# An mLSTM scan followed by a gated layer: the written-out sequence of steps is laid anew

## Chip, cores, metric

One core of one Trainium2 chip. The metric is the device time of one execution in microseconds. The kernel before takes 530.96 us, the median of 3 runs (530.82 to 531.62).

## What is computed

The reference has two stages. The first is a recurrent attention (mLSTM) over 4 batches, 8 heads, 768 steps and head size 40. The second is a gated feed-forward layer over the 3072 x 320 outputs of the first. All arrays are fp32 (the weights come as 64-bit numbers).

```python
for t in range(S):
    m_new = np.maximum(f_gate[:, :, t] + m, i_gate[:, :, t])
    f_stab = np.exp(f_gate[:, :, t] + m - m_new)
    i_stab = np.exp(i_gate[:, :, t] - m_new)
    C = f_stab * C + i_stab * outer(vt, kt)
    n = f_stab * n + i_stab * kt
    y[:, :, t] = sigmoid(o_gate[:, :, t]) * (C @ qt) / max(abs(n . qt), 1)
x = y as (B*S, H*D)                       # 3072 x 320
out = (sigmoid(x @ w_gate) * (x @ w_val)) @ w_out     # 320 -> 1536 -> 320
```

## The kernel before

The scan is done in 6 chunks of 128 steps, for 4 batches each: 24 units, counted u = 4c + b. For each unit the kernel loads q, k, v and the output gate, builds a 128 x 1024 decay matrix (`e`: exponentials on ScalarE; `em`: GpSimd masks it, L468), turns q and k round, forms scores (`b`, TensorE) and multiplies them into the decay matrix (`bm`, VectorE, L729). It gathers the values (`c`, L693), adds the carried state (`ci`, `cf`, `cs`), normalises (`cv`, `cg`, `cr`, `cx`), transposes the result (`d`) and splits it into a high and a low half (`dx`, `dy`). The state is carried by `z`, `zm`, `zd` and `za`. Units 0 to 7 turn q and k on TensorE (`a`, `ah`, and `aq`, which spreads q over a block mask, L620). Later units turn them on VectorE (`a`, L633), split them (`ah`, `al`) and send them through DRAM (`as`, then `s` and `aq`).

The gated layer works in 103 tiles (`t0` to `t102`), each with one 128-wide slice of the 1536 columns and 256 or 512 tokens. A tile has 16 matmuls up (`t`, L895), a tanh on ScalarE (`ta`, L908), the gate on VectorE (`tg`, L911), a split into high and low (`th`, `tl`; L916 or L918, and L922) and 6 or 12 matmuls down (`p`, L933). Every product is made as three products of high and low halves.

The weights come as 64-bit words and are decoded on the chip, in 30 parts (`wg`, `wv`, `wr`, `w3` to `w29`). ScalarE starts a part (`a`, L492). VectorE makes three steps on it (`b`: L497, L501 and L505), of which each reads what the one before wrote. Then `d` makes the high half (ScalarE or VectorE), `e` the low half (VectorE or GpSimd; L546, L550, L552), and `f` starts the load of a later part into a staging buffer (L513, L517, L520).

Nothing in the program plans at run time. Each step is put under a key with `put` (as `put(key + "b", ...)`), and a written string `ORDER` says which key comes next:

```python
for word in ORDER.split():
    if word == "/":
        other("pa")
        continue
    key, _, n = word.partition("*")
    for _ in range(int(n or 1)):
        f, args = todo[key].pop(0)
        f(*args)
```

So the order in the string is the order in which each engine's queue is filled; engines wait for each other by semaphores alone. A "/" swaps the next PSUM bank of two. A second table, `PARAM["eng"]`, says for a step which engine makes it ('v' VectorE, 'a' ScalarE, 'p' GpSimd). The SP queue issues almost all transfers, in the order of the string too.

Of the kernel before, what the change touches and what calls it, by code (L numbers as in the profile page):

```python
# [33 lines left out]
        'aq4.0': 'v', 'ah4.1': 'a', 'aq4.1': 'p', 'aq4.2': 'v', 'bd4': 'v', 'cr4': 'p', 'dx4': 'a', 'aq5.0': 'v',  # L34
        'ah5.1': 'a', 'bk5': 'p', 'zd5.1': 'p', 'tl1': 'p', 'tl2': 'p', 'tl10': 'v', 'arg': 'a', 'w24e': 'v',
        'w27d': 'a', 'za4.0': 'p', 'zm5.0': 'a', 'za5.0': 'p', 'zm5.1': 'a', 'ah6.0': 'a', 'ah6.2': 'v', 'aq6.2': 'v',
        'bd6': 'p', 'za6.0': 'v', 'zd6.1': 'v', 'ah7.0': 'a', 'ah7.1': 'v', 'ah7.2': 'a', 'bk7': 'p', 'cx7': 'p',
        'zm7.0': 'v', 'zd7.0': 'v', 'za7.0': 'v', 'aq8.0': 'a', 'aq8.2': 'v', 'bd8': 'v', 'cr8': 'v', 'cx8': 'p',
        'zm8.0': 'v', 'zd8.0': 'p', 'zm8.1': 'v', 'zd8.1': 'p', 'za8.1': 'v', 'aq9.0': 'a', 'e9a': 'p', 'dx9': 'v',
        'zm9.0': 'v', 'zd9.0': 'p', 'za9.0': 'p', 'zd9.1': 'v', 'aq10.0': 'a', 'cr10': 'v', 'zm10.1': 'a',  # L40
        'zd10.1': 'v', 'za10.1': 'v', 'aq11.0': 'v', 'aq11.2': 'a', 'e11a': 'a', 'bd11': 'p', 'bk11': 'p',
# [1119 lines left out]
```

## Time and profile before

| what | value |
|---|---|
| median of 3 runs | 530.96 us (530.82 to 531.62) |
| the profiled execution's own time | 532.02 us |
| its span, first to last instruction | 530.30 us |
| granted TensorE clock, mean | 0.99 |
| TensorE busy | 510.8 us (96%) |
| VectorE busy | 346.1 us (65%) |
| ScalarE busy | 196.6 us (37%) |
| GpSimd busy | 159.6 us (30%) |
| moved | 75.55 MB, mean 142 GB/s |

The profile is of one execution. A view by line groups instructions of one kind and gives the sum, the mean of one, and what ended the idle time before them. A view by stretch gives the busy time of each engine in it, with the number of instructions in brackets. In a view in order of time, each row is an instruction (or several alike) with its start and its duration in us. Durations of one engine can overlap a little, since an instruction may begin before the one ahead of it has written its last element.

### The profile page before, as it was taken

What the parts mean: (1) busy time and instruction counts of PE and PEld (TensorE: products, weight loads), DVE (VectorE), ACT (ScalarE), POOL (GpSimd) and SP (SyncE); (2) the same over time, 40 slices, a digit from 0 to 9 for tenths busy, and PEclk for the clock granted to TensorE, in tenths of its full rate; (3) what the DMA queues carried; (4) which work ended last, traced back from release to release, by engine and by line L of the source; (5) the groups of instructions that cost most, each with busy time, mean ns of one, the idle gap of its engine ahead of it and who ended that gap; (6) DMA issues with size and microseconds to landing.
All of it is one profiled execution on the core that took longest, in us unless ns stands there. A gap on an engine that the chain in (4) does not pass through costs nothing.

```text
span 530.3 us, 12170 instructions
## 1 busy us (share of the span) xinstructions
PE 510.8 (96%) x4667; PEld 461.5 (87%) x4667; DVE 346.1 (65%) x794; ACT 196.6 (37%) x514; POOL 159.6 (30%) x233
## 2 busy tenths in 40 slices
PE   7687899999999999999999999999999999999997
PEld 6476787888999999998888888888888888999997
DVE  5999999999867746675566667555655543533323
ACT  4565656773332333341243332333242140122211
POOL 4524232333643243231233414233222032111020
PEclk9978999999999999999999999999999999999999
DMA  9973866774796989496977789987777633000001
GB/s 201 240 179 128 220 154 189 175 173 75 168 198 128 228 166 200 115 163 144 196 147 170 137 191 176 206 160 176 144 171 159 132 96 88 26 27 1 12 1 39
DMA packets 227578, 75.55 MB, mean 142 GB/s; under 512 B 207040, under 2 KB 215424, under 8 KB 227520
## 3 DMA queue, kind: packets, MB, share of 16 engines
q1 hardware_dynamic: 226432, 74.51, 64.2%
q8 instruction: 37, 0.61, 0.5%
q10 hardware_dynamic: 1088, 0.26, 0.3%
q14 instruction: 21, 0.17, 0.1%
HBM read 57.61 MB, written 17.14 MB: 141 GB/s over the span
## 4 chain that ended last, share of the span: by engine, by line
PE 79%; DVE 14%; DMA 4%; issue 2%; SPq 1%; ACT 0%; DVEq 0%; ACTq 0%
PE pg L895 44%; PE po L933 22%; PE av L693 3%; PE in L744 2%; PE s L723 2%; DVE dc L505 2%; PE cs L848 2%; DVE dc L497 1%; DMA st<-in_moe_w_gate_dram 1%; DMA q<-in_q_dram 1%; DVE dc L501 1%; PE s L718 1%; PE xt L813 1%; DVE qbd L620 1%; DMA qk<-scr0q 1%
## 5 line engine op out<-in xcount | busy, mean ns | idle before, releaser
L908 ACT ACTIVATE sg<-pg 128x256 f32<-128x256 f32 (+1 forms) x103 | 48.2, 468 | 226.3 <-PE pg L895 202.4
L895 PE MATMUL pg<-xh,wh 128*128 128x256 f32 (+1 forms) x412 | 112.6, 340 | 3.1 <-ACT sg L908 2.7
L911 DVE SCALAR_TENSOR_TENSOR sg<-sg,pg 128x256 f32<-128x256 f32 (+1 forms) x103 | 53.8, 522 | 91.9 <-ACT sg L908 52.2
L895 PE MATMUL pg<-xl,wh 128*128 128x256 f32 (+1 forms) x412 | 109.6, 333 | 0.0
L895 PE MATMUL pg<-xh,wl 128*128 128x256 f32 (+1 forms) x412 | 109.4, 333 | 0.0
L922 POOL TENSOR_TENSOR gl<-sg,gh 128x256 fp32r<-128x256 f32 (+1 forms) x52 | 49.9, 960 | 152.9 <-ACT gh L916 72.2
L933 PE MATMUL po<-oh,gh 128*128 128x320 f32 x288 | 88.4, 319 | 0.0
L933 PE MATMUL po<-ol,gh 128*128 128x320 f32 x288 | 87.9, 315 | 0.0
L933 PE MATMUL po<-oh,gl 128*128 128x320 f32 x288 | 86.6, 317 | 0.0
L895 PEld LDWEIGHTS pg<-xh,wh 128*128 128x128 f32 x412 | 70.0, 190 | 9.0 <-ACT sg L908 3.3
L895 PEld LDWEIGHTS pg<-xl,wh 128*128 128x128 f32 x412 | 70.9, 190 | 6.3 <-issue 0.6
L895 PEld LDWEIGHTS pg<-xh,wl 128*128 128x128 f32 x412 | 70.1, 190 | 5.0
L895 PE MATMUL pg<-xl,w 128*128 128x256 f32 (+1 forms) x206 | 59.8, 330 | 0.0
L933 PEld LDWEIGHTS po<-oh,gh 128*128 128x128 f32 x288 | 53.4, 189 | 3.6
L933 PEld LDWEIGHTS po<-ol,gh 128*128 128x128 f32 x288 | 53.7, 188 | 2.8
L933 PEld LDWEIGHTS po<-oh,gl 128*128 128x128 f32 x288 | 53.1, 188 | 3.5 <-DVE gl L922 0.6
L895 PE MATMUL pg<-xh,w 128*128 128x256 f32 (+1 forms) x206 | 53.4, 330 | 0.1
L729 DVE TENSOR_TENSOR d<-s,d 128x384 f32<-128x384 f32 (+1 forms) x66 | 32.9, 507 | 27.3 <-PE s L723 22.1
L447 ACT ACTIVATE d<-d,at 128x128 f32<-128x128 f32 x136 | 42.4, 391 | 0.0
L916 ACT ACTIVATE gh<-sg 128x256 fp32r<-128x256 f32 (+1 forms) x53 | 26.1, 493 | 37.0 <-DVE sg L911 25.9
L468 POOL TENSOR_SCALAR_AFFINE_SELECT d<-d 128x1024 f32<-128x1024 f32 x22 | 27.0, 1229 | 39.0 <-ACT d L447 27.4
L895 PEld LDWEIGHTS pg<-xl,w 128*128 128x128 f32 x206 | 36.6, 189 | 2.3
(174 smaller groups left out, 745.9 us busy)
## 6 DMA issues: line engine op xcount, KB each, us to landing
d<-mscr SPq DMA_DIRECT2D x22, 512.0 KB
k<-in_k_dram SPq DMA_DIRECT2D x24, 160.0 KB
v<-in_v_dram SPq DMA_DIRECT2D x24, 160.0 KB
o<-in_o_gate_dram SPq DMA_DIRECT2D x24, 160.0 KB
st_o<-in_moe_w_out_dram SPq DMA_DIRECT2D x12, 320.0 KB
scr0q<-qt SPq DMA_DIRECT2D x32, 120.0 KB
scr1q<-qt SPq DMA_DIRECT2D x32, 120.0 KB
out_dram<-ob SPq DMA_DIRECT2D x24, 160.0 KB
```

The source lines that it names most:

```text
L447: nc.scalar.activation(d[:, h, :], d[:, h, :], AF.Exp, bias=at[:, c, b * H + h : b * H + h + 1], scale=-1.0)
L468: nc.gpsimd.affine_select(out=d, in_=d, pattern=[[0, H], [1, L]], compare_op=ALU.is_ge, fill=0.0, base=0, channel_multiplier=-1)
L505: nc.vector.scalar_tensor_tensor(ti, st[:, :, 0], 29, ti, ALU.logical_shift_right, ALU.bitwise_or)
L693: nc.tensor.matmul(dst[xs], lhs[:, xs], rhs, start=True, stop=True)
L723: nc.tensor.matmul(ps[g][:, m, :], ks[: 3 * D, h0 + m, :], qs[: 3 * D, h0 + m, :], start=True, stop=True)
L729: nc.vector.tensor_tensor(x, ps[g][:, :nh, :], x, ALU.mult)
L895: nc.tensor.matmul(pg[x], w[:, a, fs] if a < 2 else w[:, fs], y[c][:, a, n0:n1], start=first, stop=a == 2 and y is xl)
L908: nc.scalar.activation(sg[0], pg[0], AF.Tanh, scale=0.5)
L911: nc.vector.scalar_tensor_tensor(sg[0], sg[0], 1.0, pg[1], ALU.add, ALU.mult)
L916: nc.scalar.activation(gh[u][:, :nt], sg[0], AF.Copy)
L922: E('gl0' if c == 0 else 'gl', f'tl{n}').tensor_tensor(gl[u][:, :nt], sg[0], gh[u][:, :nt].bitcast(F32), ALU.subtract)
L933: nc.tensor.matmul(po[t], g[c, j, t0][:, (t - t0) * P : (t - t0 + 1) * P], o[:, j, :], start=j == 0 and first, stop=j == NF - 1 and last)
```

## The change

No function changes, and no step is added or taken out. Two tables differ. `ORDER` holds the same 4513 steps in another sequence: in 3677 words in place of 3647, with 39 swaps of the PSUM bank in place of 36. `PARAM["eng"]` gives another engine to 262 of the instructions: 78 go from GpSimd to VectorE and 72 back, 61 from VectorE to ScalarE and 51 back. They are splits of the gated layer (`th`, `tl`), state updates (`zm`, `zd`, `za`), low halves of weights (`w..e`), copies and normalisations. The matmuls are the same and in nearly the same sequence.

The two hunks are long; their first lines show what they are. In the lines of before, three steps of one decode often stand close (`w7b*2 w5e w7b`, `wrb*2 iq wrb`); in the new lines other VectorE steps stand between.

```diff
--- before.py
+++ after.py
@@ -26,71 +26,71 @@
     'eng': {
         'bh0': 'v', 'bh1': 'v', 'bh2': 'v', 'gl': 'v', 'gl0': 'v', 'arg0': 'a', 'q31': 'v', 'bl2': 'p', 'ca': 'v',
         'qb00': 'v', 'qb01': 'v', 'qb02': 'v', 'qb10': 'v', 'qb11': 'v', 'qb12': 'v', 'cm0': 'a', 'arg1': 'a',
-        'cm1': 'a', 'cp00': 'a', 'cp02': 'v', 'qb2': 'v', 'ro': 'v', 'xd0': 'v', 'bk0': 'p', 'cx0': 'p', 'bk1': 'p',
-        'cr1': 'v', 'cx1': 'v', 'wve': 'v', 'w3e': 'v', 'w4e': 'p', 'w5e': 'v', 'w6e': 'p', 'w7e': 'v', 'w8e': 'v',
-        'w10e': 'v', 'w11e': 'v', 'w13e': 'v', 'w16e': 'p', 'w17e': 'v', 'w18e': 'v', 'w19e': 'p', 'w20e': 'v',
-        'w21e': 'v', 'w23e': 'v', 'w25e': 'v', 'aq2.0': 'v', 'ah2.1': 'a', 'aq2.1': 'v', 'ah2.2': 'a', 'bk2': 'p',
-        'cr2': 'p', 'cx2': 'v', 'zm2.1': 'a', 'aq3.0': 'v', 'ah3.1': 'a', 'aq3.1': 'v', 'cr3': 'p', 'zm3.1': 'v',
...
+        'cm1': 'a', 'cp00': 'a', 'cp02': 'a', 'qb2': 'v', 'ro': 'v', 'xd0': 'v', 'bk0': 'p', 'cx0': 'p', 'bk1': 'p',
+        'cr1': 'v', 'cx1': 'p', 'wve': 'v', 'w3e': 'p', 'w4e': 'p', 'w5e': 'v', 'w6e': 'v', 'w7e': 'v', 'w8e': 'v',
+        'w10e': 'v', 'w11e': 'v', 'w13e': 'v', 'w16e': 'v', 'w17e': 'p', 'w18e': 'p', 'w19e': 'v', 'w20e': 'v',
+        'w21e': 'p', 'w23e': 'v', 'w25e': 'v', 'aq2.0': 'v', 'ah2.1': 'a', 'aq2.1': 'v', 'ah2.2': 'a', 'bk2': 'p',
+        'cr2': 'p', 'cx2': 'p', 'zm2.1': 'a', 'aq3.0': 'v', 'ah3.1': 'a', 'aq3.1': 'v', 'cr3': 'p', 'zm3.1': 'v',
...
@@ -102,158 +102,159 @@
 }
 ORDER = """
 w26f w25f w29f w28f w21f iw it if ii lq0 iq lk0 ib iq x0 iq x1 v1 lk1 ir lq1 ig v0 ig lv0 ig ia iq gc lo0 sp00 gc
-iac g x2 ex00 iq sp01 mk00 tr01 ig gc iq tr02 cp01 is tr00 wva wga ex01 ic igs qb01 tr11 lk2 sp10 cp00 wgb mk01 lq2
-ie cp11 cp02 sp11 lv1 qb00 ex11 lo1 bd0 qb11 tr12 sc01 x3 qb02 ex10 wgb mk11 sc00 ti01 ld2 tr10 wgb x4 / sc02 cp12
-mk10 lq3 ct0 ti00 sc11 cp10 gcs qb12 bd1 ti02 c0 bk1 ti11 v2 qb10 bk0 sc12 cg0 a2.2 iq cv0 ah2.2 z1 cv0 wvb cv0 wvb
-sc10 ct1 cr0 lk3 wvb wra iq wgf a2.1 ti10 ah2.1 ti12 c1 cx0 zm1.0 gc g wgd / d0 wrb*2 iq wrb dx0 wge cg1 wvd w3f
-dy0 wrd cv1*3 cr1 aq2.2 zm1.1 cx1 wre w5a / d1 g w3a a2.0 ld4 g*2 dx1 iq w3b ah2.0 g w3b e2 iq dy1 / a3.0 w3b t0
-w5b e2a wrf t0 wve iq lo3 t0*2 w5b t0*2 ld3 t0 w3d w5b t0 e2m t0 lv2 t0 w7a t0*2 g t0 w5d t0 lo2 t0*2 w3e h0 ta0
-lv3 aq2.1 w6a t1 h0c t1 tg0 t1*3 ah3.0 th0 im w7b*2 w5e w7b p0 w4a / z0 w6b w7d w6b p0 t1 lk6 t1 w6b t1 ct3 t1*2
-b2.2 gs bd2 w4b w6d w4f t1 w4b t1*2 w4b t1 w5f t1 w6e t1 tl0 w7f zm0.0 ta1 bm2.2 wvf e3a zm0.1 tg1 t2*2 p0 aq2.0
-t2*2 p0 t2 / a3.1 w7e th1 t2*2 ah3.1 t2 tl1 t2 g t2 e3 g a3.2 p0 t2 ah3.2 t2*3 g t2 g b2.0 ta2 e3m e4 aq3.0 p0 b2.1
-aq3.1 bm2.0 t3*2 w4d t3 t2 bm2.1 w8a b3.1 aq3.2 bk2 w11a bd3 t3 c2 bm3.1 ct2 v3 w8b w4e w8b p1 w8b b3.0 cv2*2 w8d
-w8f cg2 t3*2 bm3.0 b3.2 bk3 w9a lq4 cv2 tg2 z2 cr2 bm3.2 w6f t3 w11b c3 zm2.1 zm2.0 w8e w9b p1*2 cv3 th2 w9b t3*2
-w9b p1*2 tl2 cx2 d2 cg3 w9d w9f t3 cv3 lk4 p2 cv3 dx2 t3 w11b t3 cr3 t3 w12a w11b t3 ld5 t3*2 z3 dy2 w11d w11f
...
+iac g x2 ex00 iq sp01 mk00 tr01 ig gc iq tr02 cp01 is tr00 ex01 wga mk01 lo1 g tr11 cp02 igs sp11 bd0 cp11 lq2 ex11
+qb01 gcs tr12 wgb iq lk2 sp10 qb02 cp00 wgb cp12 qb00 sc01 ex10 qb11 lv1 tr10 wgb sc00 wra mk10 x4 ti01 cp10 sc02
+ie wva ld2 ti00 v2 mk11 wgf ti02 ct1 c0 wrb bd1 ct0 x3 qb10 bk1 wgd iq cg0 sc10 cv0 wvb ic sc11 qb12 cv0 wvb a2.1
+cv0 iq wvb bk0 ah2.1 z1 ti11 sc12 zm1.1 lk3 ti10 a2.0 cr0 wvd ti12 c1 wrb zm1.0 cx0 gc wrb wge g ah2.0 w3f a2.2 cg1
+iq ah2.2 cv1 wrd iq cv1*2 d0 lv2 wre iq aq2.2 lq3 dx0 cr1 w3a dy0 e2a w3b cx1 d1 g w3b v3 g w5a z0 w3b wve w3d wrf
+dx1 ld3 w5b w3e w7a zm0.1 lo2 dy1 t0 ld4 t0 w5b t0 lv3 w6a aq2.0 t0*2 e2 aq2.1 t0*4 w5b t0*3 a3.0 w7b t0 w5d t0 w6b
+e2m t0*2 g w7b ta0 tg0 t1*2 zm0.0 t1 th0 w6b im ah3.0 bd2 w5e w7b w4a t1 w6b t1 w4f t1 w7d t1*2 lo3 t1 w4b t1*2 w6d
+tl0 t1 h0 a3.1 w4b t1 g t1 ah3.1 t1 p0 w4b e3 t1 / b2.2 h0c aq3.1 w7f p0*2 w5f g b2.0 w6e ta1 lk6 e3a g p0 t2 w6f
+t2 tg1 t2*3 w7e t2*2 ct2 t2*2 e3m t2 w8a bm2.0 t2*2 p0 th1 t2 bm2.2 t2 / a3.2 w4d aq3.0 t2 b2.1 ah3.2 w4e tl1 p1
+w8b ta2 b3.1 bd3 bm2.1 ct3 w9a w8b p0 t3 bk2 e4 c2 bm3.1 w9b aq3.2 p1 w8b p1 b3.0 cv2 cg2 w8d w8f cv2 w11a p1 w9b
+bk3 t2 bm3.0 b3.2 lq4 t3 cv2 w11b p1 z2 cr2 wvf bm3.2 tg2 zm2.0 c3 w11b cx2 w9b th2 t3*2 cv3 zm2.1 w11b t3 w9f t3
+tl2 t3*2 lk4 d2 cv3 cg3 ld5 t3*2 cv3 dx2 t3 w8e t3*2 cr3 t3 g p2 dy2 w12a t3 p2 w9d p2 w12b t3 cx3 ta3 d3 w12b w9e
...
```

## Rows read from the trace of the kernel before

**Rows 1.** The page's busy time of engines: us, share of span, instructions.
```profile
PE 510.8 (96%) x4667; PEld 461.5 (87%) x4667; DVE 346.1 (65%) x794; ACT 196.6 (37%) x514; POOL 159.6 (30%) x233
```

**Rows 2.** Busy time by stretch; columns in its first row.
```profile
core 0: us, PE busy (x) PEld busy (x) DVE busy (x) ACT busy (x) POOL busy (x), PEclk, DMA share, GB/s
0.00:10.00 10.00, 7.50 (x35) 6.35 (x35) 4.72 (x12) 4.00 (x10) 4.40 (x21) 1.00 0.91 206
10.00:20.00 10.00, 8.88 (x112) 6.67 (x112) 9.61 (x24) 6.09 (x24) 6.05 (x11) 1.00 1.00 230
20.00:30.00 10.00, 5.88 (x88) 5.37 (x89) 9.56 (x25) 7.02 (x22) 2.01 (x2) 0.75 0.69 187
...
120.00:140.00 20.00, 19.87 (x180) 16.98 (x179) 19.05 (x41) 7.59 (x20) 8.02 (x12) 1.00 0.57 113
...
160.00:200.00 40.00, 40.00 (x440) 39.56 (x439) 26.57 (x69) 12.72 (x39) 13.06 (x24) 1.00 0.87 179
...
320.00:360.00 40.00, 40.00 (x345) 35.09 (x344) 23.38 (x50) 11.19 (x29) 12.04 (x18) 1.00 0.92 186
```

**Rows 3.** TensorE's waits over the span: us in total, times, longest.
```profile
PE xt L813 <- DVE x L791: 4.0, 1, 4.0
PE pg L895 <- ACT sg L908: 2.7, 2, 2.2
PE s L718 <- DVE d L729: 2.5, 1, 2.5
...
PE in L744 <- DMA qk<-scr0q: 0.5, 1, 0.5
```

**Rows 4.** The chain that ended last, in order of time: start, us, what.
```profile
57.88 6.97 DMA st<-in_moe_w_gate_dram
...
305.40 5.32 DMA qk<-scr0q
...
386.24 3.50 PE pg L895 x15
...
514.23 1.91 PE pg L895 x16
516.14 0.73 PE po L933 x5
```

**Rows 5.** VectorE in order of time, 35 to 37 us: start, duration, instruction.
```profile
35.02 0.42 DVE L505 SCALAR_TENSOR_TENSOR dc<-st,dc 128x256 int32<-128x256 int32 x1
35.36 0.42 DVE L497 TENSOR_SCALAR dc<-dc 128x512 f32<-128x512 f32 x1
35.81 0.43 DVE L501 TENSOR_SCALAR dc<-dc 128x512 int32<-128x512 int32 x1
36.27 0.69 DVE L505 SCALAR_TENSOR_TENSOR dc<-st,dc 128x512 int32<-128x512 int32 x1
36.88 0.17 DVE L699 COPY dl<-d 128x8 f32<-128x8 f32 x1
```

**Rows 6.** All engines in order of time, near 70 us.
```profile
69.96 1.24 POOL L468 TENSOR_SCALAR_AFFINE_SELECT d<-d 128x1024 f32<-128x1024 f32 x1 [2.77 <-ACT d L447]
...
70.17 1.31 DVE L620 TENSOR_TENSOR qbd<-qk,bmask 80x256 f32<-80x256 f32 x1
```

**Rows 7.** VectorE groups by shape, 10 to 140 us: busy, mean ns, idle before.
```profile
L505 DVE SCALAR_TENSOR_TENSOR dc<-st,dc 128x512 int32<-128x512 int32 x12 | 11.4, 948 | 0.2
...
L505 DVE SCALAR_TENSOR_TENSOR dc<-st_o,dc 128x320 int32<-128x320 int32 x12 | 5.8, 486 | 0.2
```

**Rows 8.** Line L729 over the span: ns least/median/most, first and last start.
```profile
L729 DVE TENSOR_TENSOR d<-s,d x66: 380/548/560, 39.8 to 452.4; 128x384 f32<-128x384 f32 x44, 128x256 f32<-128x256 f32 x22
```

**Rows 9.** VectorE in order of time, two landmarks.
```profile
127.39 0.49 DVE L505 SCALAR_TENSOR_TENSOR dc<-st_o,dc 128x320 int32<-128x320 int32 x1
...
130.65 0.69 DVE L911 SCALAR_TENSOR_TENSOR sg<-sg,pg 128x512 f32<-128x512 f32 x1
```

More of the change, by code (lines that the diff above doesn't have):

```diff
@@ new lines @@
+ta19 tg19 e10a p18 t20 zm7.1 lk10 t20 zm7.0 t20 th19 t20 p17 lv10 t20*4 p18 t20*2 p18 t20 za7.1 t20 o3 t20 tl19
+t20*3 cr7 p19 ta20 p19*2 al10.0 p18*2 tg20 t21 as10.3 t21 p19 cx7 t21 bd8 th20 as10.1 t21*2 e10 t21 as10.0 tl20
+t21*8 aq9 t21*2 p20 aq9 ta21 p20 / ci8 as10.2 tg21 p19*2 cf8 zd8.1 p20 th21 t22 e10m t22 a11.0 t22*6 dy6 t22*4
+za7.0 t22*2 tl21 t22 / b8.0 bk8 ta22 p20 b8.1 oh2 t22 p21 bm8.1 p20 t23*2 tg22 p21 t23*2 p20 th22 t23 bm8.0 / b8.2
+tl22 t23*2 s9 zd8.0 p21 t23*2 s9 t23 p22 bd10 t23 s9 ah11.0 t23*2 a10.1 t23 s9 t23 p22 t23 ta23 p21 al11.0 p21 d7
@@ new lines @@
+cv15 p53 cv15 aq16 p52 cg15 ta54 p53 t54 aq16 cv15 p52 p53 tg54 cr15 p53 p52*4 cx15 p52*2 p53 th54 p53*3 tl54 d15
+z15 dx15 p54 zm15.0 p54 lk18 dy15 p54*2 t55 bk16 t55 p54 bd17 zd15.0 t55*2 a18.0 t55 p54 t55 zd14.1 oh9 t55 a17.1
+t55 oh8 t55*2 o8 ah17.1 t55*2 as17.3 al17.1 t55 o9 t55*2 ld18 z16 za15.0 ta55 s16 p53 za14.1 t55 p53 zm15.1 t56
+tg55 za15.1 p54 p53 bk17 zm16.1 t56*2 th55 t56 p54*2 t56 tl55 t56*2 oh10 t56*2 o10 t56*2 lv17 t56*2 s16 t56*2
+as17.6 ci16 ta56 lo18 p55 zd16.0 aq17 p54 t56 zd16.1 as17.4 p55 t57 tg56 t57*2 cf16 p55 p54 as17.7 p55 zm16.0 p54
@@ new lines @@
+th59 p58*3 ld19 p57 p58 e18m t60 tl59 t60 p58 t60*2 bd18 t60*2 v19 t60 za16.0 t60*4 p58 t60*2 b17.0 ta60 b17.2
+bm17.0 t60 p59*2 bm17.2 t61 cg16 t61*2 tg60 t61 b17.1 t61 th60 bm17.1 s18 t61*2 aq18 ci17 tl60 s18 p59 aq18 p59
+zd17.1 p60 s18 t61*2 zd17.0 cf17 s18 t61 z17 lv19 za16.1 cr16 a20.0 t61 zm17.0 t61 a19.0 cx16 t61 lq21 t61*2 za17.0
+lo19 t61 ta61 p59 c17 ah20.0 tg61 ct17 t62 ct18 cs17 p59*3 e19a ah19.0 p59*2 cv17 t62 al19.0 p60*4 p59 as19.2 p60
+p59 th61 t62*2 cv17 ah19.1 t62 as19.0 tl61 cv17 cg17 / d16 t62 dx16 t62 aq18 t62*2 al19.1 t62 cr17 t62*2 p61*2
@@ new lines @@
+ah23.1 t73 s22 cv20 p71*2 cv20 s22 al23.1 bm21.1 t73 p71 s22 t73 cv20 tl72 t73 s22 e22m t73 as23.5 t73 bm21.2 t73*3
+p71*2 zd19.0 p71*3 cr20 p71*2 t73*2 lo23 cx20 / c21 ta73 as23.7 e23a t73 aq22 cs21 t74*2 tg73 t74 p72 ct21 p72
+as23.6 t74 e23 t74 cg21 aq23 t74 th73 t74 aq23 t74 aq23 t74 d20 lv23 t74 dx20 t74 p71 as23.4 t74 tl73 t74 aq22
+t74*2 dy20 p72*2 ta74 p72 cv21 p72 cv21 p72 p73 p72*4 t75 t74 p72 t75 tg74 t75*2 p73 th74 t75*2 cv21 tl74 t75 cr21
+p73 t75*4 za19.0 cx21 p74 t75 za19.1 t75*2 v23 t75 p73*2 ta75 p73*2 t75 d21 tg75 t76 dx21 t76*3 p73*2 t76*2 p73
@@ new lines @@
+p84 tg85 p84 t86*2 th85 t86*4 tl85 t86*9 p84 p85 ta86 t86 p84 p85 tg86 p85 t87*2 th86 t87*4 tl86 t87*2 p85 t87*7
+p86*2 ta87 p86 t87 p85*2 tg87 t88*4 th87 t88*2 tl87 t88*9 p86*2 ta88 t88 p86 p87 tg88 p87 t89*2 th88 t89*4 tl88
+t89*9 p87*2 ta89 p88*2 t89 p87*2 tg89 t90*4 th89 p88 t90 tl89 p88 t90 p88 t90*9 p88 t90 ta90 p89*3 tg90 p89 t91*2
+th90 t91*5 tl90 t91*9 p89 ta91 p89 p90*2 tg91 p90 t92*2 th91 t92*4 tl91 t92 p90 t92 p91 t92*8 p91 ta92 p91 p90*2
+tg92 p91 t93*2 th92 t93*4 tl92 t93*4 p92 t93*5 p91 t93 ta93 p92*2 oh21 p91 tg93 p92 t94*2 th93 t94*4 tl93 t94*10
@@ L257 @@
+p100 p101*2 th102 p101*2 tl102 p101*2 p102*5 oh22 p102 oh23 o22 o23
 """
```

255 lines of the change are left out of this document (115 added, 140 removed), and 120 rows, old and new, of the table PARAM.

## The prediction

> **What bounds the kernel now.** Start with the busy shares [rows 1]: TensorE is taken for 96% of the span, VectorE for 65%. A mean over stages says little, so the table by stage comes next [rows 2]. From 10 to 140 us VectorE is busy for 125 of 130 us (three of the ten stretches of that time are shown, from 95.3 to 96.1%), while TensorE is down to 5.88 of 10 us at 20 to 30 us and still short of full at 120 to 140. From 160 us on it is the reverse: TensorE is full and VectorE is busy for 26.57 of 40 us. So there are two kernels in one: an opening of some 130 us whose pace VectorE sets (weight decode, masks, score products), and then about 395 us in which TensorE runs through the gated layer. The list of TensorE's waits [rows 3] says the same: the large ones (4.0, 2.7, 2.5 us) end on VectorE or on ScalarE behind it, all in the opening; after 140 us there is one of 0.5 us. The chain of waits [rows 4] gives TensorE's spacing once it is full: 3.50 us for 15 matmuls of 512 columns (0.233 each), 1.91 for 16 of 256 (0.119), 0.73 for 5 of 320 columns (0.146). No matmul is added or dropped, so the part behind the opening costs the same before and after unless a wait appears in it. What the change is worth is therefore what VectorE saves ahead of the same TensorE step in the opening.
>
> **Three terms make VectorE's time in the opening.** The last weight word is decoded at 127.39 us [rows 9]; in the written order 273 VectorE instructions stand ahead of it. Each priced at the undisturbed duration of its shape, less the 0.08 us by which neighbours overlap, they sum to 95.9 us. 53 neighbours of which the second reads what the first wrote add 53 x 0.11 = 5.8 us. Stalls behind GpSimd add 15.7 us, and idle time, half of it in the first 10 us, 10.0. That is 127.4, the measured time; so the terms can be trusted to about 1 us. The same sums, step by step, for the change:
>
> **Dependent neighbours: -4.2 us.** Look at the starts in the VectorE rows of the decode [rows 5]. The 128x256 L505 starts at 35.02 and takes 0.42, and the unrelated L497 behind it starts at 35.36, 0.08 us before that end. L501 reads what L497 wrote and starts 0.03 us after its end (35.36 + 0.42, then 35.81), and so does L505 at 36.27. The unrelated L699 again starts 0.08 us early. A dependent neighbour thus costs 0.11 us. The written order has 54 of them ahead of the gate of tile 15 (130.65 us, [rows 9]), 30 of them the decode's L497-L501-L505; the new one has 16. 38 x 0.11 = 4.2 us. Since VectorE has no slack there, nothing hides this. The steps put between the pairs are other VectorE steps that were due anyway, so they cost nothing; a decode's result comes one step later (some 0.5 us), and ScalarE's copy behind it can wait that long, since ScalarE is busy for only 6 to 7 of 10 us [rows 2].
>
> A rule of the Trainium skill speaks against this term: "VectorE: DVE Perf Modes", section "The DRAIN you can't avoid", has every operation followed by a pipeline flush before the next starts, and says that a semaphore between two costs nothing extra. By it a dependent neighbour would cost no more than another and the sum would lose its 4.2 us. The 0.11 us of [rows 5] disagrees, so the rule is kept as a rival only.
>
> **Engine choices: -0.7 us.** The steps that change engine nearly cancel on VectorE. Ahead of the gate of tile 15 it has 276 instructions in place of 278 and the same sum without pairs (97.8 against 97.9 us); ahead of the gate of tile 13 it has 1.3 us less (86.1 against 87.4). I take the middle, 0.7; the ends are 0 and 1.3. GpSimd gets 53 tensor instructions ahead of the last decode in place of 47 (36.9 us against 34.1), and it is idle for more than half of the opening [rows 2]. Their later finish (a 128x320 subtraction takes GpSimd longer than VectorE) falls on weight parts and masks which TensorE reads several us later by the order, and GpSimd's queue has nothing urgent behind them. TensorE's own list is nearly the same: the matmul work ahead of the gates of tiles 13 and 15 goes from 79.3 to 80.1 and from 92.0 to 92.5 us. Those extra 0.5 to 0.8 us would come on top; I leave them out.
>
> **Stalls behind GpSimd: -1.5 us.** One case in full [rows 6]: GpSimd's mask runs from 69.96 to 71.20; VectorE's 80x256 product (0.41 us undisturbed) starts at 70.17 and takes 1.31, to just behind that end. It shows in the groups too: L505 on 128x512 has a mean of 948 ns, on 128x320 486 [rows 7], where the widths alone would give 690 for the first. Instructions that read a matmul's bank are never caught: L729 stays within 380 and 560 ns in all its 66 cases [rows 8]. Over all VectorE instructions before 127.39 us, 29 run over the usual duration of their shape by more than 0.1 us, 15.7 us together, 0.54 each. How many are caught after the change cannot be read from the trace. The nearest evidence is which VectorE step the order puts next behind each GpSimd step. Before the last decode that is one that works in SBUF alone (and so can be caught) 25 times with 18.3 us of GpSimd time before, and 25 times with 16.3 us after. 15.7 x 16.3 / 18.3 = 14.0, so 1.7 us less; I take 1.5. The ends lie far off: alignment to a tenth of a us decides each case and an order holds it only roughly, so anything from half of the stalls gone (-7.8) to 45 of the 53 GpSimd instructions catching one (+8.6) has to be kept.
>
> **The queues of SP and ScalarE.** Loads and saves move by a few places: the two q loads ahead of the second weight block, the mask loads. The opening's weight loads wait for a staging buffer that VectorE's decode frees (one such load, 6.97 us from its issue, is in the chain [rows 4]), so they come earlier with VectorE and I cost them at nothing as long as the transfer engines have room: 0.69 to 1.00 of their time is taken between 10 and 30 us, 0.57 between 120 and 140 [rows 2]. If that room is gone, it is the rival on transfers below.
>
> **The clock.** Between 20 and 30 us the granted clock is 0.75 on average, that is part of the stretch at 1.2 in place of 2.4 GHz, while TensorE waits (5.88 of 10 us busy) [rows 2]. VectorE is the bound there, so a shift of that piece costs or gives 1 us at most; it is in the range.
>
> **The sum.** 4.2 + 0.7 + 1.5 = 6.4 us off the opening. The profiled execution took 532.02 us, a span of 530.30 and 1.72 around it; the median of the runs is 530.96, 0.2% below that. What is saved is an absolute piece, so it comes off the median: 530.96 - 6.4 = 524.6 us. Behind the opening nothing is late next at once: VectorE, now 66% busy, has to follow a TensorE that is 6 us earlier, which it can.
>
> **Rivals.** (1) More stalls behind GpSimd: slower. The place is the opening, the price 0.54 us for each further case. The two other terms give 4.9 us, so the balance turns at 9 further cases, 38 in place of 29. With 45 of the 53 GpSimd instructions catching a VectorE step, 16 more, it is 8.6 - 4.9 = 3.7 us slower, 534.7. For it speaks that GpSimd has 2.8 us more to do there; against it, that the steps listed next are no worse than before. (2) Far fewer stalls: with half of them gone 4.9 + 7.8 = 12.7 us come off, 518.3. For it speaks that a score product (L729) or its twin of the first units stands next behind 12 GpSimd steps in place of 6; against it, that as many as before can still be caught. (3) The gain is given back to transfers. In the full stage the transfer engines are taken for 0.87 to 0.92 [rows 2], q and k go through DRAM and back, and one such load, 5.32 us long, is in the chain with TensorE waiting 0.5 us for it [rows 3, 4]. If that traffic sets a pace of its own, a TensorE that comes 6 us earlier waits 6 us more, and the time stays at 530.5 to 531. Against it: a single wait in 390 us. (4) The pairs give nothing (the rule above): 0.7 + 1.5 = 2.2 us, 528.8. The rows speak against it.
>
> **Chances.** Forecast 0.61; more stalls 0.12; far fewer 0.12; given back 0.10; pairs worth nothing 0.05. About 0.2% (1 us) is what a measurement of this kernel can tell from no change. Faster: 0.61 + 0.12 + 0.05 = 0.78; within 0.2%: 0.10; slower: 0.12. The forecast's own range is 521 to 528. The range of 8 in 10 takes in the given-back case and the nearer halves of rivals 1 and 2: 518.0 to 533.5.
>
> **What would show it.** In the changed profile the last decode (L505) should start near 121 us and the gate of tile 15 near 124.5; the rows of L497, L501 and L505 should stand apart with other steps between; TensorE's waits in the opening should shrink by some 6 us and stay under 1 us behind 140. The third term is right if the VectorE instructions over their usual duration before the last decode sum to 12 to 16 us. Wrong would be: the mean of L505 on 128x512 at or above 950 ns and that sum over 20 us (rival 1); a sum under 9 (rival 2); an earlier last decode with new waits of TensorE for loads after 140 us (rival 3); pairs gone with the last decode unmoved (rival 4).

## The result

The changed kernel takes 525.71 us (median of 4 runs, 525.08 to 526.06) where the kernel before took 530.89 beside it (4 runs, 530.74 to 531.62): a ratio of 0.9898, 95% interval 0.9881 to 0.9915. The forecast was 524.6, faster. The profiled execution of the changed kernel took 525.08 us, its span is 523.30. The two profiled executions lie 6.9 us apart, the medians 5.2: the one of before was 1.1 us above its median, the one of after 0.6 below.

All line numbers are one higher than before (L505 is now L506); in the experiments they shift by a few lines either way, because the written order takes more or fewer of them. The page's busy time, against [rows 1]:

```profile
PE 508.5 (97%) x4667; PEld 460.8 (88%) x4667; DVE 339.9 (65%) x790; ACT 199.5 (38%) x522; POOL 154.0 (29%) x227
```

Busy time by stretch of the changed kernel, columns as in [rows 2]:

```profile
core 0: us, PE busy (x) PEld busy (x) DVE busy (x) ACT busy (x) POOL busy (x), PEclk, DMA share, GB/s
10.00:20.00 10.00, 9.53 (x119) 7.24 (x117) 9.58 (x23) 7.84 (x28) 6.44 (x12) 1.00 0.98 211
20.00:30.00 10.00, 5.63 (x91) 4.64 (x91) 9.84 (x27) 7.22 (x20) 3.91 (x7) 0.83 0.78 211
100.00:120.00 20.00, 19.33 (x170) 16.68 (x170) 17.39 (x40) 11.17 (x29) 9.47 (x11) 1.00 0.71 143
120.00:140.00 20.00, 20.00 (x248) 17.80 (x247) 16.01 (x37) 7.99 (x21) 13.16 (x17) 1.00 0.69 139
160.00:200.00 40.00, 40.00 (x489) 39.55 (x476) 24.93 (x65) 14.19 (x43) 12.30 (x23) 1.00 0.91 187
```

Compare the rows of 20 to 30 and of 120 to 140 us with those of before. In the first VectorE is still full (9.84 of 10). In the second it has fallen from 19.05 to 16.01 of 20 us. But TensorE, full there now, was as good as full there before (19.87), so this stretch had next to nothing to give. Where VectorE's time counts is the point at which the prediction's reasoning was too simple; the section on why it was right or wrong takes it up.

TensorE's longest waits (us in total, times, longest), against [rows 3]:

```profile
PE xt L814 <- DVE x L792: 2.6, 1, 2.6
PE pkeep0x L995 <- DVE warm L1132: 1.3, 1, 1.3
PE av L694 <- POOL qbd L621: 1.0, 1, 1.0
...
PE pg L896 <- ACT xh L820: 1.0, 1, 1.0
```

The wait for xt is 2.6 in place of 4.0 us; the waits of 2.7 for sg and of 2.5 for d no longer stand among the long ones. From 140 us on the same view lists none.

VectorE in order of time, at 44 to 47 us of the changed kernel, against [rows 5]:

```profile
43.91 0.55 DVE L730 TENSOR_TENSOR d<-s,d 128x384 f32<-128x384 f32 x1
44.37 0.65 DVE L502 TENSOR_SCALAR dc<-dc 128x320 int32<-128x320 int32 x1
44.95 0.54 DVE L730 TENSOR_TENSOR d<-s,d 128x384 f32<-128x384 f32 x1
45.42 0.31 DVE L498 TENSOR_SCALAR dc<-dc 128x320 f32<-128x320 f32 x1
45.65 0.48 DVE L506 SCALAR_TENSOR_TENSOR dc<-st_o,dc 128x320 int32<-128x320 int32 x1
46.05 0.15 DVE L779 TENSOR_SCALAR den<-av 128x8 f32<-128x8 f32 x1
```

The decode's steps now have score products (L730) and other blocks' steps between them, and each starts 0.07 to 0.09 us ahead of the end of the one before. Its groups by shape from 10 to 140 us, against [rows 7]:

```profile
L506 DVE SCALAR_TENSOR_TENSOR dc<-st,dc 128x512 int32<-128x512 int32 x12 | 9.7, 805 | 0.0
L506 DVE SCALAR_TENSOR_TENSOR dc<-st_o,dc 128x320 int32<-128x320 int32 x12 | 6.2, 516 | 0.0
```

The wide one's mean fell from 948 to 805 ns, while the narrow one's rose from 486 to 516. The two landmarks of [rows 9] are the last decode and the gate of tile 15:

```profile
124.08 0.49 DVE L506 SCALAR_TENSOR_TENSOR dc<-st_o,dc 128x320 int32<-128x320 int32 x1
...
125.35 0.68 DVE L912 SCALAR_TENSOR_TENSOR sg<-sg,pg 128x512 f32<-128x512 f32 x1
```

### The profile page after: what moved, and what is told of

It reads as the page before. It is cut to its first block, busy times and chain, and to the rows that moved or that the text cites. A ratio compares the mean times of both kernels' runs of the same rounds, so it can differ in the third digit from the quotient of the medians.

```text
span 523.3 us, 12199 instructions
## 1 busy us (share of the span) xinstructions
PE 508.5 (97%) x4667; PEld 460.8 (88%) x4667; DVE 339.9 (65%) x790; ACT 199.5 (38%) x522; POOL 154.0 (29%) x227
## 4 chain that ended last, share of the span: by engine, by line
PE 88%; DVE 8%; issue 1%; ACT 1%; POOL 1%; POOLq 0%; DVEq 0%
PE pg L896 51%; PE po L934 24%; PE av L694 3%; PE in L745 2%; PE s L724 2%; PE cs L849 2%; PE s L719 1%; PE xt L814 1%; DVE dc L502 1%; DVE dc L506 1%; DVE gl L923 1%; DVE w L551 1%; DVE dc L498 1%; PE mb L1016 1%; DVE d L1062 0%
## 5 line engine op out<-in xcount | busy, mean ns | idle before, releaser
L896 PE MATMUL pg<-xl,wh 128*128 128x256 f32 (+1 forms) x412 | 107.8, 331 | 0.0
L934 PE MATMUL po<-oh,gl 128*128 128x320 f32 x288 | 87.8, 317 | 0.9 <-DVE gl L923 0.9
L923 POOL TENSOR_TENSOR gl<-sg,gh 128x256 fp32r<-128x256 f32 (+1 forms) x31 | 28.2, 909 | 124.7 <-DVE gh L919 69.0
L896 PE MATMUL pg<-xl,w 128*128 128x256 f32 (+1 forms) x206 | 62.4, 332 | 0.0
L923 DVE TENSOR_TENSOR gl<-sg,gh 128x256 fp32r<-128x256 f32 (+1 forms) x72 | 45.7, 634 | 17.1 <-ACT gh L917 9.5
L896 PE MATMUL pg<-xh,w 128*128 128x256 f32 (+1 forms) x206 | 55.0, 332 | 0.0
L730 DVE TENSOR_TENSOR d<-s,d 128x384 f32<-128x384 f32 (+1 forms) x66 | 32.8, 505 | 15.3 <-PE s L724 13.4
```

The source lines that it names most:

```text
L730: nc.vector.tensor_tensor(x, ps[g][:, :nh, :], x, ALU.mult)
L896: nc.tensor.matmul(pg[x], w[:, a, fs] if a < 2 else w[:, fs], y[c][:, a, n0:n1], start=first, stop=a == 2 and y is xl)
L923: E('gl0' if c == 0 else 'gl', f'tl{n}').tensor_tensor(gl[u][:, :nt], sg[0], gh[u][:, :nt].bitcast(F32), ALU.subtract)
L934: nc.tensor.matmul(po[t], g[c, j, t0][:, (t - t0) * P : (t - t0 + 1) * P], o[:, j, :], start=j == 0 and first, stop=j == NF - 1 and last)
```

## One account for all kernels

The prediction's account of VectorE ahead of the gate of tile 15 can be drawn up for each kernel that ran. "Own work" is every VectorE instruction ahead of it at the undisturbed duration of its shape, less 0.08 us each; "pairs" are dependent neighbours at 0.11 us; "stalls" are the instructions more than 0.1 us over the usual duration of their shape. "Idle" is the remainder up to the measured start, so an error in a price lands there. What is taken as the usual duration matters: with the median of each shape over all these runs the stalls of before come to 17.5 us in place of 16.1, those of after to 13.0. Differences under about 1.5 us between kernels of different order are therefore not to be leaned on. Times are us.

| kernel | gate of tile 15 | own work | pairs | stalls | idle | median |
|---|---|---|---|---|---|---|
| before | 130.65 | 97.9 | 54: 5.9 | 30: 16.1 | 10.7 | 530.89 |
| after | 125.35 | 97.8 | 16: 1.8 | 25: 13.1 | 12.6 | 525.71 |
| old_pairs_parted | 127.83 | 97.9 | 31: 3.4 | 22: 12.3 | 14.3 | 529.07 |
| new_decodes_joined | 134.08 | 97.8 | 71: 7.8 | 24: 13.4 | 15.1 | 534.48 |
| new_order_old_engines | 128.06 | 98.6 | 19: 2.1 | 23: 12.8 | 14.6 | 529.87 |
| old_order_new_engines | 130.97 | 97.4 | 49: 5.4 | 31: 16.5 | 11.7 | 533.55 |
| new_extra_early | 127.19 | 101.5 | 16: 1.8 | 24: 12.4 | 11.5 | 527.52 |
| new_extra_late | 125.11 | 97.8 | 16: 1.8 | 26: 13.2 | 12.3 | 525.95 |
| new_no_masks | 122.95 | 97.8 | 16: 1.8 | 20: 9.4 | 14.0 | 524.37 |
| new_four_moved | 123.33 | 97.8 | 16: 1.8 | 21: 11.0 | 12.8 | 522.98 |
| new_three_moved | 123.39 | 97.8 | 16: 1.8 | 22: 11.1 | 12.7 | 525.27 |
| new_three_moved_e10 | 123.05 | 97.8 | 16: 1.8 | 22: 11.0 | 12.5 | 523.21 |
| new_three_moved_e10_parted | 122.99 | 97.8 | 12: 1.3 | 22: 11.5 | 12.4 | 522.73 |

The kernel before, run beside the others, took 531.33 us with the four from old_pairs_parted to old_order_new_engines, 531.16 with the next four and 531.25 with the last three.

## The experiments

**Pairs parted in the old order.** Before's order and engines; 26 steps stand one VectorE step later (16 of them steps of the decode), so that 31 of the 54 pairs are left.

```diff
-... lk3 wvb wra iq wgf a2.1 ti10 ah2.1 ...
+... lk3 wra iq wgf a2.1 ti10 wvb ah2.1 ...
-... wrb*2 iq wrb dx0 wge cg1 wvd ...
+... wrb*2 iq dx0 wge cg1 wrb wvd ...
```

> The kernel before with 26 VectorE steps moved back by one VectorE step each, nearly all in the decode, so that 31 dependent neighbours in place of 54 stand ahead of the gate of tile 15; engines and all else as before. Theory (a dependent neighbour costs 0.11 us where VectorE sets the pace): 23 x 0.11 = 2.5 us less, 528.4 us, the gate of tile 15 near 128.1 us in place of 130.65, and a stall sum behind GpSimd that moves by chance by about 1 us. Rival (every VectorE operation is flushed anyway, so pairs are free): 530.9, unchanged.

Measured: 529.07 us (527.63 to 530.18), ratio 0.9954 (0.9941 to 0.9967), 2.3 us less. The gate of tile 15 came 2.8 us earlier for 23 pairs, 0.12 us each, near the price read from [rows 5]. But the account says that the sum is not clean: stalls fell by 3.8 us too, and idle rose by 3.6. Moving 26 steps also moves what meets GpSimd. The kernel did get faster, but this run alone does not give the price of a pair.

**Decodes joined in the new order.** After's order and engines; the three steps of 29 decodes stand together again (58 moves), which gives 71 pairs in place of 16.

```diff
-... cg0 sc10 cv0 wvb ic sc11 qb12 cv0 wvb a2.1 cv0 iq wvb bk0 ...
+... cg0 sc10 cv0 ic sc11 qb12 cv0 wvb*3 a2.1 cv0 iq bk0 ...
```

> The changed kernel with one part undone: the three VectorE steps of 29 decodes are put next to each other again, so that 71 dependent neighbours in place of 16 stand ahead of the gate of tile 15. Theory: 55 x 0.11 = 6.0 us more, less up to 2 us if fewer steps are caught behind GpSimd (the steps next behind GpSimd's hold 13.8 us of its time in place of 16.3): 529.7 to 531.7 us. Rival (pairs free, the gain came from the engine choices or the matmul order): 525.7, unchanged.

Measured: 534.48 us (533.76 to 535.05), ratio 1.0061 (1.0048 to 1.0074): 8.8 us over after, slower even than before. VectorE in order of time shows the neighbours' price again:

```profile
48.17 0.16 DVE L776 SCALAR_TENSOR_TENSOR den<-av,den 128x8 f32<-128x8 f32 x1
48.25 0.32 DVE L492 TENSOR_SCALAR dc<-dc 128x320 f32<-128x320 f32 x1
48.60 0.33 DVE L496 TENSOR_SCALAR dc<-dc 128x320 int32<-128x320 int32 x1
48.96 0.49 DVE L500 SCALAR_TENSOR_TENSOR dc<-st_o,dc 128x320 int32<-128x320 int32 x1
49.37 0.55 DVE L724 TENSOR_TENSOR d<-s,d 128x384 f32<-128x384 f32 x1
```

L492 starts 0.08 ahead of the end of the unrelated step before it; L496 and L500 start 0.03 behind the end of the step they read, and L724 is again 0.08 ahead. So 0.11 us a pair, 6.0 us for 55. The cleanest place to see it is the gate of tile 4. Ahead of it stand 26 of the 55 further pairs, 2.9 us, with about 0.2 us less of own work and 0.2 less of stalls, and it comes at 59.55 us in place of 57.05, 2.5 later. At the gate of tile 15 it is 8.7 us: stalls are the same (13.4), own work too, and idle is 2.5 us more. TensorE's waits name a part of that (us in total, times, longest):

```profile
PE po L928 <- DVE gl L917: 3.4, 2, 2.7
```

where after has 0.9 us on that line. Joining draws first steps later and last steps earlier, past gates and splits that TensorE waits for; so the order held more than the pairs, and my 4 to 6 us were too few. How much of the rest is this, no run separates.

**Each half alone.** The new order with the old engine table, and the old order with the new table.

```diff
 new_order_old_engines:
-    'eng': { ... }     # of after
+    'eng': { ... }     # of before
 old_order_new_engines: ORDER of before, 'eng' of after
```

> The new sequence with the engine table of before. Theory: ahead of the gate of tile 15 it has 19 pairs in place of 54 (-3.8 us), 0.7 us more VectorE work, and 20.9 us in place of 19.4 of GpSimd time with a step behind it that can be caught (+1.2): 529.0 us. Rival A (the engine table carries the gain): 530.9. Rival B (the sequence alone carries it, whatever the engines): 525.7.

> The sequence of before with the new engine table. Theory: 49 pairs in place of 54 (-0.5 us), 0.5 us less VectorE work, the same stalls: 529.9 us, and up to 2 us more if a step now waits for an engine it was not laid out for. Rival A (the engine table carries the gain): 525.7 to 527.

Measured: the new order alone 529.87 us (529.32 to 530.51), ratio 0.9974 (0.9963 to 0.9985), 1.5 us less than before. The new engines alone 533.55 (532.88 to 534.36), ratio 1.0044 (1.0032 to 1.0056), 2.2 us more. Together they give 5.2 less: the halves don't add. The account shows why for the first: with 0.8 us more own work, 3 more pairs and 2.0 us more idle, its gate of tile 15 comes 2.7 us behind after's. For the second it shows 49 pairs and 31 stalls at the gate of tile 15, only 0.3 us from before. At the gate of tile 24 it is still 0.3 (166.84 against 166.51 us), though 40 stalls (21.4 us) stand ahead of that gate against 36 (19.0) in before. The loss comes behind it (337.63 against 336.43 at the gate of tile 60), where TensorE's listed waits are no longer than in before (0.4 and 0.5 us); its cause is not shown. Here the new engine choices gain 4.2 us with the new order and lose 2.2 with the old one.

**More work for VectorE, early or late.** Eight maxima over a 128x384 constant, whose result nobody reads, put between VectorE steps at 36 to 108 us, or at 247 to 368 us.

```diff
+    spare = const.tile([P, 3], F32, name="spare")
+    def spare_max():
+        nc.vector.reduce_max(out=spare, in_=bmask, axis=mybir.AxisListType.X)
+    for x in range(8):
+        put("xx", spare_max)
-... p1 b3.0 cv2 cg2 w8d ...
+... p1 b3.0 xx cv2 cg2 w8d ...
```

> The changed kernel with 8 further VectorE instructions (a maximum over the 128x384 block mask into a tile that nothing reads), spread over the opening from about 34 to 108 us. By the rows of 384 columns each takes some 0.47 us net, 3.8 us together. Theory (VectorE sets the pace of the opening and what it loses there moves the end one to one): 529.5 us, the gate of tile 15 near 129 us. Rival (VectorE is no longer the bound after the change, TensorE or the loads are): 525.7 to 527.

> The changed kernel with the same 8 VectorE instructions spread over the full stage, from about 260 to 370 us. Theory (TensorE is full there and VectorE has a third of its time free): 525.7 us, unchanged within 0.5. Rival (any VectorE time moves the end): 529.5.

Measured: early 527.52 us (526.83 to 528.31), 1.8 over after; late 525.95 (524.47 to 526.76), 0.2 over after, too little to tell from none. The late one is as expected: behind the opening VectorE's time costs nothing. The early one is half of what was expected. Two of the eight in order of time, and the gates of tiles 3 and 15, in the early kernel:

```profile
46.67 0.54 DVE L363 TENSOR_REDUCE spare<-bmask 128x3 f32<-128x384 f32 x1
47.13 0.15 DVE L783 TENSOR_SCALAR den<-av 128x8 f32<-128x8 f32 x1
...
55.37 0.54 DVE L363 TENSOR_REDUCE spare<-bmask 128x3 f32<-128x384 f32 x1
55.83 0.41 DVE L916 SCALAR_TENSOR_TENSOR sg<-sg,pg 128x256 f32<-128x256 f32 x1
...
127.19 0.68 DVE L916 SCALAR_TENSOR_TENSOR sg<-sg,pg 128x512 f32<-128x512 f32 x1
```

Each takes 0.54 us and costs its queue 0.46 (the next starts at 47.13), 3.7 us for eight. The gate of tile 15 came 1.84 us later: idle shrank by 1.1 us and stalls by 0.7. But "half" is an average over two kinds. Three of the eight stand ahead of the gate of tile 3 (at 35.75, 46.67 and 55.37 us), and that gate comes at 55.83 in place of 54.34 us, 1.49 later, about what the three cost. The other five, at 65.68 to 108.40 us, add only 0.35 by the gate of tile 15, for 2.3 us of work. So a microsecond of VectorE ahead of some 57 us moves what follows by a whole one, and behind that point hardly at all: there idle time and fewer stalls take it in.

**No masks.** GpSimd's masks of units 2 to 7 are left out, so their scores keep the upper triangle.

```diff
-... w6b e2m t0*2 ...
+... w6b t0*2 ...
```

(and e3m to e7m likewise)

> The changed kernel with the GpSimd masks of units 2 to 7 (six instructions of 128x1024, 1.1 to 1.95 us each) left out, so the decay matrices of these units are not masked and the output differs. In the changed kernel's trace four VectorE steps stall behind these masks ahead of the gate of tile 15 (at 31.5, 62.7, 80.2 and 113.5 us, 0.9 us each, 3.6 together). Theory (such a stall is paid in full): 522.1 us, stall sum ahead of that gate near 9.5 us in place of 13.1. Rival A (the stalls are hidden by other waits, or other steps are caught in their place): 525.0 to 525.7. A gain over 4 us would say that the masks' own time on the way to the score products counts too.

Measured: 524.37 us (523.48 to 524.68), ratio 0.9869 (0.9855 to 0.9882), 1.3 under after, not 3.6. The stalls fell by just the 3.7 us expected (13.1 to 9.4), but idle took 1.4 and the gate of tile 15 came 2.4 us earlier. Of these, 1.4 went between the gates of tiles 18 and 20, at 138 to 146 us, as the next run shows.

**Stalls moved away.** Five VectorE steps (a decode step, three products, a split) are put elsewhere in after's order, so that four stalls behind GpSimd should go. In this order unit 3's product bm3.1 stands ahead of bd3, which copies the last column of the decay matrix: for its three heads the copy then holds products, so unit 3's weights of the carried state differ; the work is the same.

```diff
-... w8b ta2 b3.1 bd3 bm2.1 ct3 ... e4 c2 bm3.1 w9b ...
+... bm2.1 w8b ta2 b3.1 bm3.1 bd3 ct3 ... e4 c2 w9b ...
```

(also the third wvb behind ti11, bm4.0 ahead of the third w15b, and tl13 behind a9.0)

> The changed kernel with five VectorE steps moved by one to three places, so that a step that reads a matmul's bank or turns q stands where a step that works in SBUF was caught behind GpSimd in the trace (at 18.7, 42.5, 66.5 and 113.5 us). If the alignment holds, some 0.4 + 0.5 + 0.45 + 0.8 = 2.1 us of stalls go: 523.6 us. Rival (every shift re-aligns what follows, so other steps are caught): 525.7 plus or minus 1.

Measured: 522.98 us (522.86 to 524.72), ratio 0.9853 (0.9837 to 0.9869), 2.7 under after; but its profiled execution is the one of 524.72, and in that one little is gained. The gate of tile 15 is 2.0 us earlier (stalls 11.0). Then VectorE, in order of time:

```profile
140.34 1.21 DVE L636 CAST qt<-qt 128x320 fp32r<-128x320 f32 x1
141.47 1.85 DVE L778 SCALAR_TENSOR_TENSOR den<-t,den 128x8 f32<-128x8 f32 x1
143.36 0.20 DVE L781 RECIPROCAL den<-den 128x8 f32<-128x8 f32 x1
```

and GpSimd:

```profile
140.03 1.34 POOL L465 TENSOR_SCALAR_AFFINE_SELECT d<-d 128x1024 f32<-128x1024 f32 x1 [2.82 <-ACT d L444]
141.34 1.96 POOL L449 TENSOR_TENSOR d<-at,d 128x1024 f32<-128x1024 f32 x1
```

A step of 128x8 that takes 0.15 us elsewhere takes 1.85: it started 0.13 us behind GpSimd's subtraction for unit 10 (e10a) and ended 0.02 us behind it. In after the same two steps stand the other way round. VectorE:

```profile
142.36 1.21 DVE L640 CAST qt<-qt 128x320 fp32r<-128x320 f32 x1
143.50 0.15 DVE L782 SCALAR_TENSOR_TENSOR den<-t,den 128x8 f32<-128x8 f32 x1
143.68 0.20 DVE L785 RECIPROCAL den<-den 128x8 f32<-128x8 f32 x1
```

and GpSimd:

```profile
143.71 1.90 POOL L453 TENSOR_TENSOR d<-at,d 128x1024 f32<-128x1024 f32 x1 [0.31 <-DVE den L782]
```

There the subtraction came 0.21 us behind the small step and cost VectorE only 0.65 us at a later cast. The profile of new_no_masks has the same catch of 1.69 us at 141.09. So what is gained ahead of 125 us can be lost at 141.

**Three moves, and the subtraction taken off GpSimd.** The same without the move of bm3.1 (four steps, three stalls), so that the computation is the whole one; then with unit 10's subtraction in ScalarE's exponentials; then with 12 further steps moved by one VectorE step.

```diff
 new_three_moved: the five moves above without bm3.1
 new_three_moved_e10:
-        'e10a': 'p'
+        'e10a': 'a'
 new_three_moved_e10_parted:
-... w23b w21d t11 w23b t11 lv7 a8.0 t11 ...
+... w23b w21d t11*2 lv7 a8.0 w23b t11 ...
```

> The changed kernel with three of the four moves of the run before, and without the one that brought unit 3's product ahead of the copy of the last column (bd3): the third step of wv goes behind ti11, bm2.1 goes ahead of w8b, bm4.0 ahead of the third w15b, tl13 behind a9.0 (four words, three stalls in place of four). Theory of the stalls: the stalls of VectorE before the gate of tile 15 go from 13.1 us to 11 to 11.5, and the gate comes 1.5 to 2 us earlier (123.4 to 123.9 in place of 125.35). How much of it arrives at the end hangs on what GpSimd's subtraction e10a (1.9 us, 'd<-at,d', near 141 to 145 us) catches: in the run with four moves it caught the small product of cv7 for 1.69 us, in the changed kernel a cast for 0.65. If it catches cv7 again, the end is 524.5 to 525.5; if not, 523.5 to 524. Rival, stalls count one to one to the end: 523.7 at any rate.

> The same, and the subtraction of unit 10 (e10a, GpSimd, 1.9 us) is made on ScalarE in the exponentials' bias, as the kernel does for other units (e10 with it: two groups of four exponentials of 0.39 us in place of one of 1.04 over all heads, about 2.1 us more for ScalarE, which is busy for a third of the time there). Theory of the stalls: nothing on GpSimd can catch VectorE between 143 and 146 us, so the gain at the gate of tile 15 arrives: 0.7 to 1.7 us under the run with three moves, 523 to 524. Rival, ScalarE becomes late there (its tanh of tiles 18 to 20 behind the longer exponentials): 525 or more, with waits of TensorE or VectorE on ScalarE in 140 to 160 us.

> The same with further dependent neighbours parted: 12 ahead of the gate of tile 15 in place of 16, 104 in all in place of 119. At 0.11 us each: 0.4 us less at that gate, so 0.3 to 0.5 us under the run without it if the stalls stay as they are; pairs behind 140 us are worth nothing since TensorE is full there. Rival, any shift of the order makes new stalls: within plus or minus 1 us.

Measured: three moves 525.27 us (523.53 to 525.67), ratio 0.9891 (0.9874 to 0.9907); with e10a on ScalarE 523.21 (522.88 to 524.06), 0.9852 (0.9836 to 0.9868); parted further 522.73 (522.48 to 522.81), 0.9839 (0.9825 to 0.9854). The gate of tile 15 came at 123.39 us with the three moves, 2.0 us earlier than in after, as expected, and the median gained 0.4. Its profiled execution is its best one (523.53); GpSimd in it:

```profile
140.09 1.34 POOL L465 TENSOR_SCALAR_AFFINE_SELECT d<-d 128x1024 f32<-128x1024 f32 x1 [2.83 <-ACT d L444]
142.16 1.90 POOL L449 TENSOR_TENSOR d<-at,d 128x1024 f32<-128x1024 f32 x1 [0.73 <-DMA d<-mscr]
```

Here the subtraction waited 0.73 us for its load and caught a cast for 1.07 us in place of the small step for 1.69. The other three executions, at 525.05 to 525.67, have no profile; that they had a costlier catch fits, but it was not seen. With the subtraction off GpSimd the median fell by 2.1 us and no VectorE step that starts between 141 and 150 us is caught. The rival, a late ScalarE, did not show. The last step, 0.5 us, is as expected, but the intervals of these two overlap; in the account its 0.5 us of pairs is met by 0.5 us of stalls. This last kernel is faster than both: 522.73 against 525.71 and 531.25. Its page's busy time and two stretches:

```profile
PE 508.2 (98%) x4667; PEld 460.8 (88%) x4667; DVE 336.9 (65%) x790; ACT 200.9 (39%) x529; POOL 152.0 (29%) x226
```

```profile
0.00:60.00 60.00, 51.62 (x541) 43.48 (x542) 52.88 (x137) 39.29 (x112) 25.59 (x50) 0.94 0.81 212
60.00:140.00 80.00, 79.41 (x710) 69.06 (x709) 71.43 (x168) 46.96 (x120) 38.08 (x48) 1.00 0.72 168
```

TensorE is idle for 8.4 us of the first 60 and for 0.6 of the next 80; what is left to gain lies ahead of 60 us.

## Why the prediction was right, and where it was not

**The forecast's case is the one that came about.** 525.71 lies in the forecast's own range of 521 to 528, and its three terms are seen in the account: -4.1 us of pairs (forecast -4.2), -0.1 of engine choices (-0.7), -3.0 of stalls (-1.5). With 1.9 us more idle the gate of tile 15 comes 5.3 us earlier, against 6.4. That the sum of the terms came so near is in part luck, because they were summed to the wrong place.

**What bounds the kernel** was right for the first 60 us and wrong behind. "Since VectorE has no slack there, nothing hides this" is the step that failed, and with it the opening of 130 us. A full VectorE does not say that TensorE waits for it. The first 60 us and the next 80, before and then after, columns as in [rows 2]:

```profile
0.00:60.00 60.00, 45.82 (x495) 38.58 (x496) 52.43 (x126) 33.87 (x97) 23.77 (x46) 0.91 0.76 190
60.00:140.00 80.00, 78.57 (x634) 66.35 (x634) 77.28 (x174) 49.09 (x127) 26.78 (x35) 1.00 0.67 161
```

```profile
0.00:60.00 60.00, 50.11 (x534) 42.50 (x534) 52.59 (x134) 38.01 (x108) 25.44 (x50) 0.94 0.81 211
60.00:140.00 80.00, 78.75 (x697) 67.66 (x698) 71.78 (x167) 46.08 (x120) 37.97 (x47) 1.00 0.71 162
```

TensorE's idle time of the first 60 us fell from 14.2 to 9.9 us. From 60 to 140 us it was 1.4 us before and is 1.3 after: there was almost nothing to gain, in before as in after, though VectorE was busy for 77.28 of the 80 us. The 19.87 of 20 us that the prediction read as "still short of full" is full but for 0.13 us. The landmarks say the same. The gate of tile 4, before and after:

```profile
63.38 0.42 DVE L911 SCALAR_TENSOR_TENSOR sg<-sg,pg 128x256 f32<-128x256 f32 x1 [0.21 <-PE pg L895]
```

```profile
57.05 0.40 DVE L912 SCALAR_TENSOR_TENSOR sg<-sg,pg 128x256 f32<-128x256 f32 x1
```

It comes 6.3 us earlier, nearly all of the 6.9 by which the two profiles differ at the end. (The gates behind it, up to tile 15, come 4.6 to 7.3 us earlier; up to 18 matmuls more or fewer stand ahead of them.) Estimated from the traces as in the account, but with the median durations, the 6.3 us are 25 of the 38 parted pairs (2.8 us), about 1.7 us of stalls, and about 1.8 us of VectorE's own work: 127 of its instructions stand ahead of that gate in place of 135. The last term is in no sum of the prediction, since at the gate of tile 15 it is gone (276 against 278). The other 13 pairs lie where TensorE no longer waits. The maxima of new_extra_early show it from the other side. The room behind 60 us has an end, though: in new_decodes_joined TensorE is busy for only 73.44 of the 80 us.

**Dependent neighbours** had the right price, but were counted over too long a stretch. The rows of new_decodes_joined and its 2.5 us at the gate of tile 4 show the price; old_pairs_parted moved the same way, with fewer stalls as well. So the rival at 528.8 us, pairs worth nothing, does not hold. It rested on the rule of the Trainium skill ("VectorE: DVE Perf Modes", section "The DRAIN you can't avoid") that a semaphore between two operations costs nothing extra; the rows here differ from it by 0.11 us. Not every late start is a pair, though. The subtractions of L551, on 64 of the 128 partitions each, start 0.01 to 0.03 us behind the end of the step ahead in all eight cases of after's first 140 us, and read nothing that it wrote. The account leaves this in idle.

**Engine choices** were costed by their own sum, which hardly moved. Yet without them the new order is 4.2 us slower than after (529.87 against 525.71). At the gate of tile 15 it is 2.7 us, mostly idle time (2.0), not stalls (12.8 us against 13.1). Where the rest goes is not shown.

**Stalls behind GpSimd** were mis-sized, within their bounds: 25 cases and 13.1 us ahead of the last decode, where 14.2 was forecast and 12 to 16 called right. The proxy, the next step in the written order, had the sign. Rivals 1 and 2 (over 20 us, under 9) are excluded, and the mean of L506 on 128x512 is 805 ns, not 950.

**The gain was not given back.** TensorE's waits behind 140 us vanished, 0.5 us in [rows 3] and none now. Ahead of the gate of tile 15 TensorE is idle for 15.6 us before and 11.1 after. That is 4.5 us less, where "some 6" was forecast.

**The clock** was looked at between 20 and 30 us alone. Two more stretches, before and then after:

```profile
40.00:50.00 10.00, 7.41 (x100) 5.99 (x101) 9.66 (x21) 6.28 (x20) 4.67 (x6) 0.95 0.39 137
50.00:60.00 10.00, 8.74 (x113) 7.39 (x113) 9.08 (x26) 5.20 (x15) 3.77 (x5) 0.88 0.69 174
```

```profile
40.00:50.00 10.00, 8.83 (x169) 6.90 (x168) 9.97 (x27) 6.45 (x20) 6.18 (x8) 1.00 0.61 167
50.00:60.00 10.00, 8.74 (x69) 8.13 (x69) 9.79 (x26) 5.96 (x15) 3.08 (x4) 1.00 0.81 252
```

Before falls a second time to the lower level, 1.2 GHz, near 50 us, with TensorE busy for 7.41 of the 10 us ahead of that; after, busier there, does not. TensorE's busy time over the span is 2.3 us less (510.8 to 508.5) for the same 4667 matmuls. How much of that reaches the end no run separates, as VectorE sets the pace in the same stretch.

**The last decode** was expected near 121 us and started at 124.08. It stands later in the new order (97.0 us of own work ahead of it in place of 95.9), and 2.3 us more idle lie ahead of it. A step that changes its place in the order is a poor landmark; the gate, 125.35 against 124.5, was a good one.

**The base** mattered too. The profiles show 6.9 us, the medians 5.2. The forecast, 6.4 us off the median, is 1.2 us above the gain of the medians and 0.5 below that of the profiles.

## What to carry over

Put an independent step between each dependent pair on VectorE where TensorE waits for that engine, and count the pairs there: 0.11 us each here. That VectorE is full does not show that TensorE waits for it: look first at TensorE's own idle time, stretch by stretch, and sum the savings only up to where it ends. A known piece of work, added at several places, tests this: here three pieces ahead of that point came through whole and five behind it hardly at all. A long GpSimd operation can cost VectorE 0.65 us in one execution and 1.51 in another with the same steps up to there (after and new_extra_late, at 143 to 147 us). Making it on an engine with room was worth 2.1 us here.

## What was not expected of the hardware

What a GpSimd instruction costs VectorE depends on tenths of a microsecond, and a transfer can decide it: one subtraction cost VectorE 0.65 (after), 1.07 (new_three_moved), 1.51 (new_extra_late) or 1.69 us (new_four_moved) according to its start, and in the second of these it was released by its load. That fits the rule of the Trainium skill ("SBUF — State Buffer", section "Who interferes with whom") that whichever of the two issues first holds the shared pair of ports for its whole instruction. The same section of the Trainium skill says that reductions never contend on this chip: the 16 added ones took 498 to 548 ns, with five of them beside a running GpSimd instruction, which agrees.

The scale of a catch was new too: a step of 0.15 us took 1.85, twelve times its own length, and ended 0.02 us behind the GpSimd instruction. So it is the length of that instruction that counts, not that of the step it catches.
